# The low parts of w_out and of the experts' weights, from GpSimd to VectorE

## The chip, the cores and the metric

The kernel runs on one core of a Trainium2 chip. The metric is device time in microseconds (us) of one execution. Names used below: PE is TensorE (matmuls), DVE is VectorE, ACT is ScalarE, POOL is GpSimd, SP is SyncE, which here issues the DMAs from HBM. GpSimd issues the indirect DMAs (gathers and stores by token number) itself.

## What is computed

Three layers in a row, in float32: a gated linear attention, a mixture of experts with a capacity of 384 tokens per expert, and a dense feed-forward layer.

```python
# attention, per batch and head (4 x 8 x 768 x 48)
state = f[:, :, t, :, None] * state + k_t (outer) v_t;  y[:, :, t] = q_t @ state
# experts: N=3072 tokens, D=384, E=8, F=1024; tokens are taken in order of logit, 384 each
for e in range(E):
    h = np.maximum(x[mask] @ w1[e], 0.0)
    out[mask] = h @ w2[e]
# dense layer, d_ff=2048
h = x @ w_in
g = h * np.clip(h + 3.0, 0.0, 6.0) / 6.0
return g @ w_out
```

w_in and w_out arrive as float64; the other tensors as float32.

## The kernel before

**Precision.** Each float32 matrix of the feed-forward part is kept as two: a rounded "high part" (float32r, made by a copy on ACT) and a "low part", the difference between the value and its high part. A product is three matmuls: high x high, low x high, high x low (`run_passes`, L672 to L675; `wih`/`wil`, `woh`/`wol{g}`, `w1h`/`w1l`, `w2h`/`w2l`, `xh`/`xl`, `hh`/`hl`). `split_raw` (L668) makes both parts: L669 the copy on ACT, L670 the subtraction on the engine that it is given.

**Stages.** First attention with the routing's first steps (to about 213 us), in which w_in is also prepared; then eight expert stages, one per expert, in which the 384 tokens of an expert go through w1, w2, w_in and w_out (`Experts.ffn_`: l1, l2, l3, l4). An expert stage is a generator of some 144 ticks; a tick is one `run_passes`, three matmuls of 128x128 by 384 columns. After every tick the main loop (L978 to L989) lets other generators go one step, so their instructions land in the engines' queues between the expert's own. Queues run in program order; there is no planner, the order is that of the ticks.

**What runs beside the first expert.** `w0` is `load_weights(0)`, the rest of expert 0's weights: one step on every even tick. `out_parts` is `prep_out`, a `narrowed` generator over 16 pieces of w_out (128x384): one step on every odd tick. A piece's steps: `L872` `absolute` of the next piece on ACT, `L882`, `L884`, `L886`, `L889` on DVE (float64 words to float32), `split_raw` with its low part on GpSimd, and `fetch(i+2)`, a load on SP into the buffer `pw` (two buffers, so it waits until the low part of piece i has read its buffer). Eight steps of `out_parts` are taken ahead of the stage (`GAP`). `ap` is the routing of the next experts: DVE operations and small PE matmuls in turn (`q_ge`, `q_ok`, `q_qc`, L450 to L660).

**What runs beside every expert but the last.** `load_weights(n+1)`, from tick 42 or as soon as the expert's number is known, one step every 4 to 6 ticks (`wp`): 14 pieces (six of w1, 128x512; eight of w2, 128x384), each `split_raw` with the low part on GpSimd and `fetch(i+WLAG)` into `wst` (three buffers, WLAG=3). Expert 0's first four low parts are on DVE (`W0_DVE`). What steps are left at the end of a stage are run then. `gather(n+1)` issues three indirect loads on GpSimd; `make_x` transposes the tokens; l4's end issues three indirect stores on GpSimd.

**The expert's own vector work.** In l1 `L771` (ACT, `hh`) and `L772` (DVE, `hl`, two ticks later); in l3 `L805` (ACT), `L806` (DVE, `ga`), `L808` (ACT, `hh`), `L809` (DVE, `hl`), one block of four operations per six ticks; between l2 and l3 `L790` (ACT, `xh`) and `L791` (DVE, `xl`).

Of the kernel before, what the change touches and what calls it, by code (L numbers as in the profile page):

```python
# [10 lines left out]
F32=mybir.dt.float32; F32R=mybir.dt.float32r; BF=mybir.dt.bfloat16; I32=mybir.dt.int32; U32=mybir.dt.uint32  # L11
# [654 lines left out]
DM=384; F1=1024; F2=2048  # L666

def split_raw(nc, raw, hi, lo, eng_lo):  # L668
    nc.scalar.copy(hi, raw)  # L669
    eng_lo.tensor_tensor(out=lo, in0=raw, in1=hi.bitcast(F32), op=OP.subtract)  # L670
# [6 lines left out]
W0_DVE=(0,1,2,3); WLAG=3  # L677

class Experts:
# [15 lines left out]
    def load_weights(s,k):  # L695
        nc=s.tc.nc
        e=nc.sync.value_load(s.rt.eid[k][0:1,0:1],min_val=0,max_val=7)
        w1h=s.ew.tile([128,3,F1],F32R,name="w1h"); w1l=s.ew.tile([128,3,F1],F32R,name="w1l")
        w2h=s.ew2.tile([128,8,DM],F32R,name="w2h"); w2l=s.ew2.tile([128,8,DM],F32R,name="w2l")
        s.W[k]=((w1h,w1l),(w2h,w2l))  # L700
        jobs=[]
        for hf in range(2):
            for d in range(3):
                c=slice(hf*512,(hf+1)*512)
                jobs.append((s.w1[bass.ds(e,1),d*128:(d+1)*128,c].rearrange("a p f -> p (a f)"),w1h[:,d,c],w1l[:,d,c],512))
        for g in range(8):
            jobs.append((s.w2[bass.ds(e,1),g*128:(g+1)*128,:].rearrange("a p m -> p (a m)"),w2h[:,g],w2l[:,g],DM))
        got=[]; big=[]
        def fetch(i):
            src,_,_,n=jobs[i]  # L710
            if k>0 or i in (9,10): t=s.act.tile([128,512],F32,name="wst",bufs=WLAG)
            elif i<6:
                if i%2==0: big.append(s.act.tile([128,3,DM],F32,name=["xh","xl","xh"][i//2]).rearrange("p a b -> p (a b)"))
                t=big[i//2][:,(i%2)*512:(i%2)*512+512]
            else: t=big[1 if i<9 else 2][:,(i-6)%3*DM if i<9 else (i-11)*DM:][:,:DM]
            nc.sync.dma_start(t[:,:n],src)
            got.append(t[:,:n])
        for i in range(WLAG if k else 6): fetch(i)
        yield
        for i,(_,hi,lo,n) in enumerate(jobs):  # L720
            yield
            split_raw(nc,got[i],hi,lo,nc.vector if k==0 and (i in W0_DVE) else nc.gpsimd)
            for j in ([i+WLAG] if k else {3:(6,7,8,9,10),5:(11,12,13)}.get(i,())):
                if j<len(jobs): fetch(j)
    def gather(s,k):
        nc=s.tc.nc; ids=s.rt.ids[k]
        xg=s.act.tile([128,3,DM],F32,name="xg",bufs=1)
        for h in range(3):
            nc.gpsimd.indirect_dma_start(out=xg[:,h],out_offset=None,in_=s.x,in_offset=bass.IndirectOffsetOnAxis(ap=ids[:,h:h+1],axis=0))
        s.xg=xg  # L730
# [115 lines left out]
def gla_moe_ffn(tc,q,k,v,f_logit,moe_w_gate,moe_w1,moe_w2,moe2_w_in,moe2_w_out,out):  # L846
    nc=tc.nc
    with ExitStack() as ctx:
# [9 lines left out]
        def narrowed(pool,jobs,W,work,places):  # L858

            words=jobs[0].dtype!=F32  # L860
            got={}; mag={}
            def fetch(i):
                if i>=len(jobs): return
                n=jobs[i].shape[-1]
                w=pool.tile([128,W,2],U32,name="pw",bufs=2)
                if not words: w=w.rearrange("p c t -> p (c t)")[:,:n].bitcast(F32)
                nc.sync.dma_start(w.rearrange("p c t -> p (c t)") if words else w,jobs[i].bitcast(U32) if words else jobs[i])
                got[i]=w
            def absolute(i):
                if not words or i>=len(jobs): return  # L870
                mag[i]=work(i)
                nc.scalar.activation(mag[i],got[i][:,:,1].bitcast(F32),AF.Abs)  # L872
            fetch(0); fetch(1)
            yield
            absolute(0)
            for i in range(len(jobs)):
                yield
                r=got[i]
                if words:
                    V=nc.vector  # L880
                    lw,hw=got[i][:,:,0],got[i][:,:,1]; m=mag[i]; t=m.bitcast(U32)
                    V.tensor_scalar(m,m,2.0**-15,None,op0=OP.max)  # L882
                    yield
                    V.tensor_scalar(t,t,3,0x3ffffff8,op0=OP.logical_shift_left,op1=OP.bitwise_and)  # L884
                    yield
                    V.scalar_tensor_tensor(t,hw,0xC0000000,t,op0=OP.bitwise_and,op1=OP.bitwise_or)  # L886
                    yield
                    absolute(i+1)
                    V.scalar_tensor_tensor(lw,lw,29,t,op0=OP.logical_shift_right,op1=OP.bitwise_or)  # L889
                    r=lw.bitcast(F32)  # L890
                hi,lo=places(i)
                split_raw(nc,r,hi,lo,nc.gpsimd)
                fetch(i+2)
        def prep_in(pool):
            cc=lambda i: slice(i%4*512,i%4*512+512)
            return narrowed(pool,[moe2_w_in[i//4*128:i//4*128+128,cc(i)] for i in range(12)],512,
                            lambda i: pool.tile([128,512],F32,name="pm",bufs=2),
                            lambda i: (wih[:,i//4,cc(i)],wil[:,i//4,cc(i)]))
# [44 lines left out]
        def pools(c):  # L943
            act=c.enter_context(tc.tile_pool(name="act",bufs=2))
            pf=c.enter_context(tc.tile_pool(name="pf",bufs=4,space=PS))
            pa=c.enter_context(tc.tile_pool(name="pa",bufs=1,space=PS))
            rt.ps=c.enter_context(tc.tile_pool(name="pr",bufs=1,space=PS))
            return Experts(tc,rt,moe_w1,moe_w2,x_dram,out,ident,(wih,wil),(woh,wol),(ew,ew2,act,pf,pa))
        with ExitStack() as c:
            ex=pools(c)  # L950
            po=c.enter_context(tc.tile_pool(name="po",bufs=1))
            out_parts=prep_out(po)
            next(out_parts); w0=None
            rt.bank=None
            for i,_ in enumerate(p0):
                if got: break
                if known and w0 is None: w0=ex.load_weights(0); next(w0)
                ex.warm(WP[min(i,len(WP)-1)])
                for _ in range(GAP.get(i,0)): next(out_parts)
            ex.gather(0)  # L960
            for _ in range(3): next(w0)
            for _ in range(GAP['ids']): next(out_parts)
            for _ in range(4): next(w0)
            ex.warm(WARM2)
            ex.make_x0(WARM3)
            for _ in range(W0N): next(w0)
            def all_phases():
                for _ in p0: yield
                for n in range(1,E):
                    for w in rt.phase(n):  # L970
                        for _ in range(w): yield
            ap=all_phases()
            def spread(g):
                for w in g:
                    for _ in range(w): yield
            for n in range(E):
                wgen=xgen=None; gat=n+1>=E; gi=None; last=n+1>=E
                for i,_ in enumerate(ex.ffn(n)):  # L978
                    if n==0:
                        if i%2==0: next(w0,None)  # L980
                        else: next(out_parts,None)
                    if not (PAUSE if n else PAUSE0)[0]<=i<(PAUSE if n else PAUSE0)[1] and (n or i>=P1): next(ap,None)
                    if last: continue
                    if wgen is None and len(known)>n+1 and i>=W_SLOT: wgen=ex.load_weights(n+1); wi=i; wp=max(WPMIN,min(WPMAX,(138-i)//15))
                    if not gat and len(got)>n+1 and i>=30:
                        ex.gather(n+1); gat=True; gi=i
                    if xgen is None and gat and i>=min(max(gi+X_LAG,X_SLOT),122): xgen=spread(ex.make_x(n+1))
                    if xgen is not None: next(xgen,None)
                    if wgen is not None and (i-wi)%wp==0: next(wgen,None)  # L989
                if not last:  # L990
                    while len(got)<=n+1: next(ap)
                    if not gat: ex.gather(n+1)
                    if wgen is None: wgen=ex.load_weights(n+1)
                    for _ in wgen: pass
                    if xgen is None: xgen=spread(ex.make_x(n+1))
                    for _ in xgen: pass
# [39 lines left out]
```

## Time and profile before

| | |
|---|---|
| median of 3 runs | 896.9 us (895.48 to 900.68) |
| the profiled execution | 900.39 us, its span 898.7 us |
| mean granted TensorE clock in it | 0.968 |
| PE busy | 837.9 us, 93% |
| DVE busy | 534.9 us, 60% |
| ACT busy | 371.1 us, 41% |
| POOL busy | 307.8 us, 34% |

Busy times are unions of an engine's instructions in the profiled execution. In the rows further down a timeline row is: start and duration in us, engine, line of the kernel, operation, output<-input, shape, count; in brackets how long the engine stood idle before it and what it waited for. In a table by stretches each engine has its busy us and, in brackets, its instructions; then the granted PE clock (1.00 is full), the DMA engines' busy share and GB/s. A table of waits has the waiting engine and instruction, what released it, total us, number of waits and the longest.

### The profile page before, as it was taken

To read this page: it belongs to the slowest core of one execution; us is meant where nothing else is said; L and a number is where in the kernel's file an instruction comes from. 1 tells how busy PE (TensorE), PEld (TensorE's weight loads), DVE (VectorE), ACT (ScalarE), POOL (GpSimd) and SP (SyncE) were. 2 spreads that over 40 slices of the span, in tenths; PEclk is the share of its full clock that TensorE was granted. 3 is DMA by queue.
4 is the path that set the end of the run, shared out by engine and by line. 5 is a ranking of instruction groups with operands and counts; after the bars stand their busy time and mean duration, and the time that the engine had idled before them with its cause. 6 is when DMAs were issued, how large, how long until landed. Compare 5 with 4: busy or idle time off the path is not lost.

```text
span 898.7 us, 16095 instructions
## 1 busy us (share of the span) xinstructions
PE 837.9 (93%) x6086; PEld 788.9 (88%) x6086; DVE 534.9 (60%) x1369; ACT 371.1 (41%) x741; POOL 307.8 (34%) x378
## 2 busy tenths in 40 slices
PE   7998889896987699999999999999999999999995
PEld 5887778786877699989999999999999999999995
DVE  7989799567768844674574565555674422431331
ACT  4655556424234441542354144316423541642331
POOL 7677566316213540432133133313330440331001
PEclk9999899977999899999999999999999999999998
DMA  8775686026123411120221112201220220110000
GB/s 257 189 167 125 172 237 144 29 78 187 53 71 101 119 62 37 63 71 27 74 62 33 63 62 63 71 27 58 61 77 12 75 91 18 60 47 27 1 1 31
DMA packets 77158, 71.91 MB, mean 80 GB/s; under 512 B 29200, under 2 KB 65040, under 8 KB 77072
## 3 DMA queue, kind: packets, MB, share of 16 engines
q1 hardware_dynamic: 74000, 61.37, 24.0%
q0 software_dynamic: 3072, 9.44, 3.3%
q8 instruction: 49, 0.80, 0.4%
q14 instruction: 37, 0.30, 0.1%
HBM read 61.35 MB, written 9.44 MB: 79 GB/s over the span
## 4 chain that ended last, share of the span: by engine, by line
PE 57%; issue 14%; DVE 7%; ACT 2%; POOL 2%; DMA 2%; SPq 0%; POOLq 0%; ACTq 0%; DVEq 0%
PE pF L673 9%; PE acc L673 9%; PE pF L675 8%; PE pF L674 8%; PE acc L675 8%; PE acc L674 8%; POOL wol L670 1%; DVE ga L806 1%; PE pM L195 1%; PE pA L135 1%; DMA pw<-in_moe_w_out_dram 1%; PE pY L169 1%; PE pY L163 1%; PE acc L383 1%; POOL out_dram L838 1%
## 5 line engine op out<-in xcount | busy, mean ns | idle before, releaser
L806 DVE SCALAR_TENSOR_TENSOR ga<-ga,pF 128x384 f32<-128x384 f32 x128 | 70.7, 552 | 109.5 <-ACT ga L805 109.3
L673 PE MATMUL pF<-xh,wih 128*128 128x384 f32 x384 | 133.3, 347 | 1.9 <-ACT xh L790 1.9
L673 PE MATMUL acc<-woh,hh 128*128 128x384 f32 x384 | 134.2, 349 | 0.0
L675 PE MATMUL pF<-xl,wih 128*128 128x384 f32 x384 | 131.3, 342 | 0.0
L674 PE MATMUL pF<-xh,wil 128*128 128x384 f32 x384 | 130.9, 341 | 0.0
L674 PE MATMUL acc<-woh,hl 128*128 128x384 f32 x384 | 130.0, 339 | 0.9 <-DVE hl L809 0.9
L675 PE MATMUL acc<-wol,hh 128*128 128x384 f32 x384 | 130.0, 338 | 0.0
L670 POOL TENSOR_TENSOR w1l<-wst,w1h 128x512 fp32r<-128x512 f32 x42 | 55.6, 1323 | 173.9 <-ACT w1h L669 173.9
L805 ACT ACTIVATE ga<-pF,three 128x384 f32<-128x384 f32 x128 | 74.1, 579 | 99.2 <-PE pF L675 99.1
L809 DVE TENSOR_TENSOR hl<-ga,hh 128x384 fp32r<-128x384 f32 x128 | 72.8, 569 | 60.2 <-ACT hh L808 59.9
L808 ACT CAST hh<-ga 128x384 fp32r<-128x384 f32 x128 | 65.7, 513 | 104.0 <-DVE ga L806 104.0
L670 POOL TENSOR_TENSOR w2l<-wst,w2h 128x384 fp32r<-128x384 f32 x58 | 59.9, 1035 | 111.5 <-ACT w2h L669 111.5
L771 ACT ACTIVATE hh<-pF 128x384 fp32r<-128x384 f32 x64 | 31.4, 492 | 123.1 <-PE pF L675 111.9
L772 DVE SCALAR_TENSOR_TENSOR hl<-pF,hh 128x384 fp32r<-128x384 f32 x64 | 35.5, 555 | 75.1 <-ACT hh L771 74.8
L673 PEld LDWEIGHTS pF<-xh,wih 128*128 128x128 f32 x384 | 73.0, 190 | 2.3 <-ACT xh L790 2.2
L674 PEld LDWEIGHTS acc<-woh,hl 128*128 128x128 f32 x384 | 72.7, 189 | 1.3 <-DVE hl L809 1.3
L675 PEld LDWEIGHTS pF<-xl,wih 128*128 128x128 f32 x384 | 73.3, 191 | 0.4 <-DVE xl L791 0.3
L674 PEld LDWEIGHTS pF<-xh,wil 128*128 128x128 f32 x384 | 73.2, 191 | 0.0
L673 PEld LDWEIGHTS acc<-woh,hh 128*128 128x128 f32 x384 | 72.7, 189 | 0.1
L675 PEld LDWEIGHTS acc<-wol,hh 128*128 128x128 f32 x384 | 72.6, 189 | 0.0
L673 PE MATMUL pF<-xh,w1h 128*128 128x384 f32 x192 | 67.8, 353 | 0.6 <-ACT xh L741 0.6
L675 PE MATMUL acc<-hl,w2h 128*128 128x384 f32 x192 | 64.5, 336 | 3.0 <-DVE hl L772 3.0
(286 smaller groups left out, 1766.8 us busy)
## 6 DMA issues: line engine op xcount, KB each, us to landing
wst<-in_moe_w_dram SPq DMA_DIRECT2D x58, 192.0 KB, 2.4
wst<-in_moe_w_dram SPq DMA_DIRECT2D x42, 256.0 KB, 2.7
pw<-in_moe_w_in_dram SPq DMA_DIRECT2D x12, 512.0 KB, 4.0
pw<-in_moe_w_out_dram SPq DMA_DIRECT2D x16, 384.0 KB, 3.1
v<-in_v_dram SPq DMA_DIRECT2D x24, 192.0 KB, 5.2
x_dram<-y SPq DMA_DIRECT2D x24, 192.0 KB, 3.6
fr<-in_f_logit_dram SPq DMA_DIRECT2D x7, 576.0 KB, 5.4
kr<-in_k_dram SPq DMA_DIRECT2D x7, 576.0 KB, 5.6
```

The source lines that it names most:

```text
L135: nc.tensor.matmul(pA[j][s][:,p],KH[u][r,p,c*C:(c+1)*C],QT[u][r,p,c*C:(c+1)*C],start=True,stop=True)
L163: for r in rows: nc.tensor.matmul(PY[j][p//2][r,p],St[j%2][r,p],QT[u][r,p,cc],start=p==0 or last and p==2,stop=False)
L670: eng_lo.tensor_tensor(out=lo, in0=raw, in1=hi.bitcast(F32), op=OP.subtract)
L673: nc.tensor.matmul(out, ahi, bhi, start=start, stop=False)
L674: nc.tensor.matmul(out, alo, bhi, start=False, stop=False)
L675: nc.tensor.matmul(out, ahi, blo, start=False, stop=stop)
L771: nc.scalar.activation(hh,p,AF.Relu)
L772: s.defer(2,lambda: nc.vector.scalar_tensor_tensor(hl,p,0.0,hh.bitcast(F32),op0=OP.max,op1=OP.subtract))
L805: nc.scalar.activation(a,p,AF.Relu,bias=s.three[:,0:1])
L806: late(f,1,lambda: nc.vector.scalar_tensor_tensor(g,a,6.0,p,op0=OP.min,op1=OP.mult))
L808: late(f,1,lambda: nc.scalar.copy(gh,g))
L809: late(f,3,lambda: nc.vector.tensor_tensor(out=gl,in0=g,in1=gh.bitcast(F32),op=OP.subtract))
```

## The change

Low parts go from GpSimd to DVE, one step behind the copy on ACT that makes the high part:

- in `load_weights`, a step makes piece i's high part (ACT) and piece i-1's low part (DVE), and then issues the load that waits for that low part; one more step at the end makes the last low part. Expert 0's first six pieces stay as they were (four on DVE, two on GpSimd).
- in `narrowed`, the 16 pieces of w_out (`W==DM`) take one step more each: copy, `yield`, low part on DVE and load. The 12 pieces of w_in, during attention, keep GpSimd.
- in the main loop `out_parts` goes one step on every odd tick and on every sixteenth (0, 16, ...).

```diff
@@ load_weights
+        def low(i):
+            _,hi,lo,n=jobs[i]
+            nc.vector.tensor_tensor(out=lo,in0=got[i],in1=hi.bitcast(F32),op=OP.subtract)
+            for j in ([i+WLAG] if k else ()):
+                if j<len(jobs): fetch(j)
         for i,(_,hi,lo,n) in enumerate(jobs):
             yield
-            split_raw(nc,got[i],hi,lo,nc.vector if k==0 and (i in W0_DVE) else nc.gpsimd)
-            for j in ([i+WLAG] if k else {3:(6,7,8,9,10),5:(11,12,13)}.get(i,())):
-                if j<len(jobs): fetch(j)
+            if k==0 and i<6:
+                split_raw(nc,got[i],hi,lo,nc.vector if i in W0_DVE else nc.gpsimd)
+                for j in {3:(6,7,8,9,10),5:(11,12,13)}.get(i,()): fetch(j)
+            else:
+                nc.scalar.copy(hi,got[i])
+                if i>(0 if k else 6): low(i-1)
+        yield
+        low(len(jobs)-1)
@@ narrowed
-                split_raw(nc,r,hi,lo,nc.gpsimd)
-                fetch(i+2)
+                if W!=DM:
+                    split_raw(nc,r,hi,lo,nc.gpsimd)
+                    fetch(i+2)
+                else:
+                    nc.scalar.copy(hi,r)
+                    yield
+                    nc.vector.tensor_tensor(out=lo,in0=r,in1=hi.bitcast(F32),op=OP.subtract)
+                    fetch(i+2)
@@ gla_moe_ffn
                         if i%2==0: next(w0,None)
-                        else: next(out_parts,None)
+                        if i%2 or i%16==0: next(out_parts,None)
```

## Rows read from the trace of the kernel before

**Rows 1.** Busy times by stretch: first expert in four, then the second.

```profile
213.65:235.00 21.35, 16.50 (x77) 15.18 (x77) 20.56 (x51) 7.25 (x16) 10.73 (x10) 0.84 0.26 81
235.00:282.20 47.20, 41.36 (x235) 37.51 (x236) 31.19 (x89) 18.68 (x40) 8.62 (x9) 0.96 0.22 67
282.20:313.40 31.20, 20.31 (x114) 18.72 (x112) 28.64 (x72) 12.92 (x27) 17.07 (x14) 0.87 0.45 133
313.40:329.17 15.77, 15.77 (x86) 14.53 (x86) 7.37 (x20) 8.30 (x20) 8.59 (x10) 0.83 0.17 51
329.17:412.08 82.91, 81.51 (x497) 77.81 (x497) 48.83 (x141) 31.07 (x63) 23.83 (x26) 1.00 0.17 53
```

**Rows 2.** PE's waits in the first expert's stage, 213.65 to 329.17.

```profile
PE pR L462 <- DVE q_ge L450: 8.4, 4, 5.4
...
PE acc L675 <- DVE hl L772: 3.0, 1, 3.0
...
PE pR L630 <- DVE q_qj L627: 0.3, 1, 0.3
```

**Rows 3.** PE's waits from 329.17 to 880.

```profile
PE pR L462 <- DVE q_ge L450: 1.4, 1, 1.4
...
PE pR L452 <- DVE q_qc L464: 0.7, 1, 0.7
```

**Rows 4.** Timelines of GpSimd and DVE in A.

```profile
214.09 1.97 POOL L670 TENSOR_TENSOR w2l<-xl,w2h 128x384 fp32r<-128x384 f32 x2 [1.26 <-ACT w2h L669]
...
214.11 1.02 DVE L574 TENSOR_TENSOR q_oh<-r_e,q_ec 128x16 bf16<-128x16 f32 x1
...
217.21 0.18 DVE L579 TENSOR_TENSOR q_nw<-q_nw,q_ec 128x24 f32<-128x24 f32 x1
...
232.18 1.06 DVE L884 TENSOR_SCALAR wol<-wol 128x384 uint32<-128x384 uint32 x1
```

**Rows 5.** Timelines of DVE, GpSimd and PE in C.

```profile
283.10 0.35 DVE L882 TENSOR_SCALAR wol<-wol 128x384 f32<-128x384 f32 x1
...
285.10 1.27 DVE L605 SCALAR_TENSOR_TENSOR q_sl<-q_inc,pR,q_mem 128x24 int32<-128x24 f32 x1
...
303.67 4.21 DVE L882 TENSOR_SCALAR wol<-wol 128x384 f32<-128x384 f32 x1
...
303.20 1.32 POOL L670 TENSOR_TENSOR w1l<-wst,w1h 128x512 fp32r<-128x512 f32 x1
...
306.66 0.99 POOL L670 TENSOR_TENSOR w2l<-wst,w2h 128x384 fp32r<-128x384 f32 x1
...
311.59 0.23 PE L462 MATMUL pR<-q_oh,q_ge 128*128 128x32 bf16 x2 [5.42 <-DVE q_ge L450]
```

**Rows 6.** ACT's longest wait in the first expert's stage.

```profile
ACT wol L872 <- DMA pw<-in_moe_w_out_dram: 26.5, 10, 4.1
```

**Rows 7.** Timelines of GpSimd, ACT and PE in B.

```profile
236.15 1.03 POOL L670 TENSOR_TENSOR wol<-pw,woh 128x384 fp32r<-128x384 f32 x1 [3.14 <-ACT woh L669]
...
257.03 1.15 POOL L670 TENSOR_TENSOR wol<-pw,woh 128x384 fp32r<-128x384 f32 x1 [4.10 <-ACT woh L669]
...
240.45 0.55 ACT L872 ACTIVATE wol<-pw 128x384 f32<-128x384 f32 x1 [3.99 <-DMA pw<-in_moe_w_out_dram]
...
252.26 0.44 PE L673 MATMUL pF<-xh,wih 128*128 128x384 f32 x1 [1.90 <-ACT xh L790]
```

**Rows 8.** Timeline of DVE: its subtractions of 384 and of 512 columns.

```profile
364.37 0.56 DVE L809 TENSOR_TENSOR hl<-ga,hh 128x384 fp32r<-128x384 f32 x1 [0.58 <-ACT hh L808]
364.85 0.55 DVE L806 SCALAR_TENSOR_TENSOR ga<-ga,pF 128x384 f32<-128x384 f32 x1
...
208.93 1.41 DVE L670 TENSOR_TENSOR w1l<-xl,w1h 128x512 fp32r<-128x512 f32 x2
```

**Rows 9.** Timeline of DVE in the second expert's stage.

```profile
387.72 1.36 DVE L809 TENSOR_TENSOR hl<-ga,hh 128x384 fp32r<-128x384 f32 x1
```

**Rows 10.** Timeline of DVE ahead of the first expert.

```profile
199.22 0.81 DVE L559 SCALAR_TENSOR_TENSOR q_base<-q_mx,q_st,q_b 128x1 f32<-128x1 f32 x1
```

## The prediction

> **What bounds the kernel now.** The page's busy shares come first (the table above): PE is busy 93% of the span, DVE 60%, GpSimd (POOL) 34%. Work moved from GpSimd to DVE can only pay where PE is not full, so the next view is the one by stage [rows 1]. In the second expert's stage PE is full (81.51 of 82.91 us). The first expert's, 213.65 to 329.17, takes 115.5 us, 32.6 us more. I cut it into A (213.65 to 235), B (to 282.2), C (to 313.4) and D (to 329.17). DVE fills A (20.56 of 21.35 us) and C (28.64 of 31.2), has 16 us free in B, and half of D. The table of PE's waits in that stage [rows 2] says who is late: ten rows, 21.9 us in all, of which 18.7 end with DVE (8.4 on `q_ge`, 3.0 on `hl`, seven rows down to 0.3), 2.5 with ACT, 0.7 with a DMA. For the rest of the kernel the same table has three rows, 3.0 us [rows 3].
>
> Why is DVE late? Two things stand in the timelines. In A [rows 4] a comparison of 128x16 takes 1.02 us, a subtraction's neighbour of 128x24 only 0.18. The slow one lies beside a GpSimd low part (two in 1.97 us from 214.09) and ends with it. Ten such stand in A, from 214.11 to 232.18; against the same lines elsewhere they cost 7.6 us. In C there are six [rows 5], from `L605` (1.27 us) to `L882`, which takes 0.35 us at 283.10 and 4.21 us at 303.67, while GpSimd runs four low parts in a row from 303.20 to 307.65. All six cost 7.9 us. PE then waits 5.42 us, and its granted clock is 0.87 in C and 0.83 in D, for a part of the time the lower of its two levels (1.2 instead of 2.4 GHz) [rows 1].
>
> The second thing is a loop in B. ACT's queue stops at `L872` for the next piece of w_out: 26.5 us in ten waits in this stage [rows 6]. That load starts only when GpSimd has read the buffer: its low part ends at 237.18, `L872` starts at 240.45, 3.27 us later [rows 7]. Five low parts from 236.15 to 257.03 are 5.22 us apart; 1.03 of it is the low part, and the remaining 0.92 `L872` and the copy. The program wants one each 8 ticks of the expert's loop; the second expert runs its 144 ticks in 82.91 us, 0.576 each, so 8 take 4.6 us. The loop is slower than PE, and ACT holds everything behind it (`hh`, `xh`, `ga`): PE's 1.90 us wait for `xh` before 252.26 is of this kind.
>
> **The change, part by part.** GpSimd loses low parts of 1.03 us (384 columns) and 1.32 us (512), which nobody waits for except through these two effects. DVE gains for each 128x384 0.48 us (it takes 0.56, but the next instruction starts 0.48 later), for each 128x512 0.70 us (two in 1.41) [rows 8]. The first stage gets 15 of w_out (7.2 us), 8 of expert 0 (3.8) and 14 of expert 1 (6x0.70+8x0.48=8.0): 19 us, against 15.7 us of stretching that goes (7.6+7.9, and 0.2 in B). DVE's total hardly moves. What counts is where it falls.
>
> A: out 7.6; in 8 of expert 0 (3.8), two of w_out (1.0), two more preparation steps from the doubled call at ticks 0 and 16 (0.9, of 0.35 to 0.55 each). I give the stage's end the net, -1.9. Ends: 0 (the lows queue ahead of `hl` and `q_ge`, for which PE waits) and -3.5 (the 3.0 us wait goes, and some of the slow clock, 0.84 in A).
>
> B: the loop becomes 0.92 (`L872`, copy) + 0.55 (low part, if DVE gets to it in time) + 3.27 (load) = 4.7 us. The program now gives a job 5 steps at 9 per 16 ticks, 8.9 ticks, 5.1 us at 0.576. So ACT's waits should nearly vanish. PE has 41.36 us of work in these 47.2, and the slow clock (0.96) is worth 1.9 of it: at best -7.7. DVE's work rises from 31.2 to 36.8 (8 lows 3.8, four more steps 1.8); were its idle 16 us all to stay, B would be 52.8, +5.6. I take -4, a B of 43.2 us with DVE 85% full, since the rows in which DVE idles there follow ACT's waits for the load.
>
> C: out 7.9, in four lows of w_out (1.9), two steps (0.9), seven of expert 1 (4.7): -0.4. Ends -4 (the single stall ahead of the 5.42 us wait weighs more than spread lows) and +2 (the chain through `q_ge` meets several lows). D: 7 us of lows and late steps on DVE's 7.37, in 15.77 us, hidden behind PE's matmuls, whose l4 inputs are made four blocks ahead; if that cover is gone, +2. Its clock was lost in C's long stall; all of it would be 2.7 us (0.17 of 15.77), I take -1.
>
> Experts 2 to 7: 8 us of lows per stage on a DVE that is busy 48.83 of 82.91 us, each queued one step (4 to 6 ticks) behind its copy, so it seldom waits; behind it stand `ga`, `hl` and the routing. The stretched rows are there too: `hl` 1.36 us at 387.72 [rows 9], and behind it PE's longest wait of these stages, 1.4 [rows 3]. Of the 3.0 us I take half: -1.5 (ends -3 and +1.5). An expert's load is issued one step later, since SP waits for DVE's low part: two steps, at least 8 ticks or 4.6 us, are left for 256 KB where w_out's 384 KB take 3.27, so nothing; one that misses holds ACT's queue for about 1 us. The step more at the end of expert 1's weights falls behind the first stage's last tick; those columns are used some 40 ticks later: nothing.
>
> Ahead of the stage: `L559`, on the path to the first token list, takes 0.81 us beside a low part [rows 10], where a 128x24 operation takes 0.18 [rows 4]: -0.6. The third w_out load is issued some 8 us later, behind DVE's low part and so beside the first gather; at worst it takes half of its 3.27 us from it, +1.5. Together 0. GpSimd's later gathers and stores lose the low parts queued ahead of them; PE's one wait on a gather in the first stage is 0.7 us: nothing.
>
> Sum: -1.9-4-0.4-1-1.5+0 = -8.8 us. Against the profiled execution, 900.39 us (span 898.7), that is 891.6; that execution lies 3.5 us above the median of 896.9, and from the median the sum gives 888.1. I say **889.5**, near the mean of the four executions (898.4) less the sum.
>
> On the lock itself: the Trainium skill, "SBUF — State Buffer", section "Who interferes with whom", says that DVE and GpSimd hold a shared port pair for one whole instruction while the other blocks. Read so, `L882` would have lost at most the rest of one low part, about 1.3 us, and C 5.4 us in all instead of 7.9, so that C would end 2.5 us worse than my term, an estimate inside its ends. The row shows four low parts long, and I keep the row.
>
> **Rivals.** *DVE is the new bound (slower).* Place: B. If the 16 us that DVE idles there are latency (`ga` to `hh` to `hl` pass through ACT) and not the loop, the added 5.6 us lie end to end with the rest. It decides from the point where DVE's idle time in B stays above 10.4 us (47.2-36.8). At the full 16: B +5.6, A -1.9, C +1, D +2, rest 0, so +6.7: about 905. For it: DVE already ends most of PE's waits, and 19 us are more than 15.7. Against it: ACT's 26.5 us of waits for the load. On its side, in a sentence apart: the Trainium skill, "Perfetto Trace Analysis", section "Optimizing Scalar/DVE Operations", advises taking work off a saturated DVE, to GpSimd too, though it doubts the gain because the two share a port; this change goes the other way.
>
> *Even trade (no change).* A and C give their 2.3 us, B's shorter loop is eaten by DVE's queue, the clock stays: -2 to -4, 893 to 897.
>
> *More than forecast.* The stalls were also what dropped the clock, and B runs at PE's pace: -3.5-7.7-4-2.7-3 = -20.9, some 878.
>
> **How the numbers follow.** Forecast case (882 to 892) 0.46, more 0.12, even trade 0.25, slower 0.17. A measurement of this kernel tells about 0.5% (4.5 us) from no change: faster than 892.4 0.58, between 0.25, above 901.4 0.17. The ends of all terms add to about -21 and +13; the range, 877 to 903, takes in the best case and leaves out part of the slower one.
>
> **What would show it.** Right: no DVE row on 128x24 or less above 0.3 us after 214; `L882` at 0.35 us everywhere; ACT's waits for the w_out load far below 26.5 us; PE's waits in the first stage down from 21.9 to about 13; that stage near 108 us, DVE some 3 us busier in it. Wrong: DVE over 90% busy through B and PE waiting longer for `q_ge` and `hl` there, or ACT's waits for the load unchanged because DVE reaches the low part late.

## The result and the profile after

| | before | after |
|---|---|---|
| median | 896.52 us (895.48 to 900.68) | 887.62 us (887.29 to 888.67) |
| ratio after/before | | 0.9899, interval 0.9868 to 0.9929 |
| the profiled execution, its span | 900.39, 898.7 us | 887.29, 885.6 us |

The changed kernel is 1.0% faster, 8.9 us by the medians; the sum in the prediction was 8.8. The terms of that sum are another matter, and most of what follows is about them.

The first part of the profile's page of the kernel after has each engine's busy time, share of the span and instructions. GpSimd falls from 307.8 to 169.5 us, DVE rises from 534.9 to 566.4, PE is busy 94%:

```profile
PE 831.6 (94%) x6086; PEld 783.5 (88%) x6086; DVE 566.4 (64%) x1491; ACT 372.4 (42%) x741; POOL 169.5 (19%) x256
```

The table by stretches of the kernel after, columns as in [rows 1]: the first expert's stage cut at its matmul passes 23, 88 and 122 (A to D), then the second expert's.

```profile
210.02:228.71 18.69, 16.54 (x78) 15.28 (x79) 17.89 (x62) 7.08 (x16) 0.00 (x0) 0.80 0.18 55
228.71:274.41 45.70, 40.56 (x227) 37.01 (x228) 32.33 (x92) 18.26 (x37) 0.00 (x0) 0.93 0.21 64
274.41:302.61 28.20, 20.25 (x122) 18.63 (x122) 25.26 (x80) 13.27 (x27) 2.96 (x4) 0.95 0.49 148
302.61:319.11 16.50, 15.30 (x86) 14.06 (x86) 13.63 (x35) 9.53 (x22) 1.33 (x3) 0.88 0.24 71
319.11:400.46 81.35, 81.35 (x497) 77.75 (x497) 51.28 (x156) 31.26 (x63) 6.39 (x10) 1.00 0.18 54
```

To compare equal work, the kernel before is cut at the same passes here (the cuts of [rows 1] lie within 1.3 us of these):

```profile
213.65:235.27 21.62, 16.71 (x78) 15.31 (x79) 20.72 (x51) 7.43 (x17) 10.73 (x10) 0.84 0.25 80
235.27:280.98 45.71, 39.92 (x227) 36.16 (x228) 30.46 (x87) 17.50 (x38) 8.62 (x8) 0.96 0.23 70
280.98:313.39 32.41, 21.52 (x121) 19.93 (x121) 29.20 (x74) 13.92 (x29) 17.08 (x14) 0.87 0.43 128
313.39:329.17 15.78, 15.78 (x86) 14.54 (x86) 7.38 (x20) 8.31 (x20) 8.59 (x10) 0.83 0.17 51
```

All lengths in the table below are differences of such starts, read from PE's timeline of each profiled execution; "2 to 7" runs from the start of the second stage to the start of the eighth.

| kernel | A | B | C | D | stage | 2 to 7 |
|---|---|---|---|---|---|---|
| before | 21.6 | 45.7 | 32.4 | 15.8 | 115.5 | 483.0 |
| after | 18.7 | 45.7 | 28.2 | 16.5 | 109.1 | 480.0 |

Three stretches fall: A by 2.9, C by 4.2, the later stages by 3.1. B, from which the prediction took the largest term, doesn't move at all (at a granted clock of 0.93 instead of 0.96), and D is 0.7 longer. That makes 9.5 us. DVE's busy time falls by 2.8 us in A and by 3.9 in C, nearly as much as these stretches themselves. The two spans differ by 13.1. Of the rest, 4.3 us lie in the attention part, whose instructions the change doesn't touch (its last `L200` copy starts at 188.73 before and at 184.40 after), and 0.7 us go the other way between that copy and the stage's start. The median difference of 8.9 fits 9.5 less 0.7.

PE's waits in the kernel after, first in the first expert's stage (210.02 to 319.11, three of nine rows, 16.9 us in all; ten rows and 21.9 us before, of which [rows 2] has three), then in all later ones, where one row of 0.3 us is left of three with 3.0 [rows 3]:

```profile
PE pR L462 <- DVE q_ge L450: 6.9, 5, 1.9
PE pR L452 <- DVE q_qc L464: 2.7, 3, 1.2
PE pF L760 <- DMA xg<-x_dram,q_ids: 1.8, 2, 1.2
...
PE pR L452 <- DVE q_qc L464: 0.3, 1, 0.3
```

In the kernel after, lines from `L735` on have numbers higher by 10: its `L892` is `L882` of before, `L882` is `L872`, `L899` is `L889`; `L906` and `L908` are the copy and the low part of w_out, `L731` and `L722` those of the experts.

The stretched DVE rows of A and C are gone. The timeline of DVE after has the same instructions as [rows 4], [rows 5] and [rows 10]: the comparison of 128x16 in 0.17 instead of 1.02 us, `L605` in 0.24 instead of 1.27, the clamp of w_out (`L892`) in 0.35 instead of 4.21, `L559` in 0.22 instead of 0.81. In PE's timeline the wait of 5.42 us for `q_ge` in C is gone; the longest two for it there are now 1.49 and 1.29.

```profile
194.15 0.22 DVE L559 SCALAR_TENSOR_TENSOR q_base<-q_mx,q_st,q_b 128x1 f32<-128x1 f32 x1
...
211.88 0.17 DVE L574 TENSOR_TENSOR q_oh<-r_e,q_ec 128x16 bf16<-128x16 f32 x1
...
277.54 0.24 DVE L605 SCALAR_TENSOR_TENSOR q_sl<-q_inc,pR,q_mem 128x24 int32<-128x24 f32 x1
...
300.00 0.35 DVE L892 TENSOR_SCALAR wol<-wol 128x384 f32<-128x384 f32 x1
...
300.14 0.24 PE L462 MATMUL pR<-q_oh,q_ge 128*128 128x32 bf16 x2 [1.29 <-DVE q_ge L450]
...
302.54 0.23 PE L462 MATMUL pR<-q_oh,q_ge 128*128 128x32 bf16 x2 [1.49 <-DVE q_ge L450]
```

In B nothing got quicker. The table of ACT's waits in the first stage after has 20.8 us at the load of w_out, where [rows 6] has 26.5. ACT's timeline after has three starts of `L882` (the wait for the next load of w_out), DVE's has the low parts of the same pieces:

```profile
ACT wol L882 <- DMA pw<-in_moe_w_out_dram: 20.8, 10, 5.1
...
229.63 0.56 ACT L882 ACTIVATE wol<-pw 128x384 f32<-128x384 f32 x1 [3.29 <-DMA pw<-in_moe_w_out_dram]
...
236.73 0.55 ACT L882 ACTIVATE wol<-pw 128x384 f32<-128x384 f32 x1 [5.08 <-DMA pw<-in_moe_w_out_dram]
...
241.39 0.55 ACT L882 ACTIVATE wol<-pw 128x384 f32<-128x384 f32 x1 [3.29 <-DMA pw<-in_moe_w_out_dram]
...
231.51 0.55 DVE L908 TENSOR_TENSOR wol<-pw,woh 128x384 fp32r<-128x384 f32 x1
...
237.75 0.56 DVE L908 TENSOR_TENSOR wol<-pw,woh 128x384 fp32r<-128x384 f32 x1 [2.25 <-ACT woh L906]
...
242.78 0.56 DVE L782 SCALAR_TENSOR_TENSOR hl<-pF,hh 128x384 fp32r<-128x384 f32 x1 [1.99 <-ACT hh L781]
243.25 0.55 DVE L908 TENSOR_TENSOR wol<-pw,woh 128x384 fp32r<-128x384 f32 x1
```

The low parts start 6.24 and 5.50 us apart here, and seven of them from 231.51 to 268.18 are 6.1 us apart; GpSimd's eight in B, from 236.15 to 276.77, were 5.8 apart. The prediction's loop was 4.7. Two things were missing in it: the low part at 243.25 stands in DVE's queue behind `hl` (242.78), which waits for ACT, and the load after the low part at 231.51 (done at 232.06) is there for ACT only at 236.73, 4.67 us later instead of 3.27. The distance of 6.1 us does not say by itself that the loop sets B's pace: B's 65 ticks take 0.70 us each, so the 8.9 ticks per piece of the new program are 6.2 us, and the 8 ticks of the kernel before are 5.6. The pieces keep step with the ticks in both.

### The profile page after: what moved, and what is told of

Same layout as the page of the kernel before. It is cut to its first block, busy times and chain, and to the rows that moved or that the text cites. A ratio compares the mean times of both kernels' runs of the same rounds, so it can differ in the third digit from the quotient of the medians.

```text
span 885.6 us, 15975 instructions
## 1 busy us (share of the span) xinstructions
PE 831.6 (94%) x6086; PEld 783.5 (88%) x6086; DVE 566.4 (64%) x1491; ACT 372.4 (42%) x741; POOL 169.5 (19%) x256
## 4 chain that ended last, share of the span: by engine, by line
PE 59%; issue 10%; DVE 9%; DMA 3%; ACT 3%; POOL 1%; SPq 0%; POOLq 0%; ACTq 0%; DVEq 0%
PE acc L673 9%; PE pF L673 9%; PE acc L675 9%; PE acc L674 9%; PE pF L675 9%; PE pF L674 9%; DMA pw<-in_moe_w_out_dram 2%; DVE ga L816 1%; PE pM L195 1%; DVE hl L819 1%; PE pA L135 1%; ACT ga L815 1%; PE pY L169 1%; PE pY L163 1%; POOL out_dram L848 1%
## 5 line engine op out<-in xcount | busy, mean ns | idle before, releaser
L848 POOL DMA_INDIRECT out_dram<-ga,q_ids x24 | 23.7, 989 | 430.5 <-ACT ga L846 427.4
L673 PE MATMUL acc<-hh,w2h 128*128 128x384 f32 x192 | 65.9, 343 | 0.6 <-ACT hh L781 0.6
L674 PE MATMUL pF<-xh,w1l 128*128 128x384 f32 x192 | 65.4, 341 | 0.0
```

The costliest lines, as they stand in the source:

```text
L673: nc.tensor.matmul(out, ahi, bhi, start=start, stop=False)
L674: nc.tensor.matmul(out, alo, bhi, start=False, stop=False)
L848: st=nc.gpsimd.indirect_dma_start(out=s.out,out_offset=bass.IndirectOffsetOnAxis(ap=ids[:,t:t+1],axis=0),in_=o,in_offset=None)
```

## The experiments

The theory at the outset: GpSimd's reads of SBUF hold DVE, so it pays to take its low parts away, and w_out's low parts pay most, through the loop in B. The rivals: the gain is that of the experts' low parts alone; or what counts is who computes the low part in time, and not who reads beside DVE. Each ratio is against the kernel before on the same chip (897.2 us for the first four, 896.7 for the next four, 897.5 for the last three). The kernel after has its own such ratio, 0.9899, and is best compared with them by it.

**One: the low parts of w_out alone.** The experts' low parts go back to GpSimd.

```diff
 in load_weights, against after
-                nc.scalar.copy(hi,got[i])
-                if i>(0 if k else 6): low(i-1)
+            split_raw(nc,got[i],hi,lo,nc.vector if k==0 and (i in W0_DVE) else nc.gpsimd)
```

> Only w_out's low parts go to DVE; the experts' stay on GpSimd as in the kernel before. Theory (a stretched DVE row beside a GpSimd low part is what the change removes): the stretched rows beside the experts' low parts come back, 7 of 10 at the start of the first stage, most of those before the long stall, and PE's waits of 3.0 us in the later stages; 887.6 +2 +3 +2.7, so 893 to 896. Rival (what counts is w_out's loop through ACT and its steadier steps, not the stretching): the whole gain is here already, 887 to 889.

Measured: 899.95 us, ratio 1.0028 (1.0004 to 1.0051). Both theories missed: this half of the change gives nothing and costs a little. By the table of stretches of this kernel, D (its last quarter) has DVE at 12.37 us and takes 18.03, where before it took 15.78. Part of that is PE's granted clock, 0.76 instead of 0.83, which this one execution doesn't separate from DVE's part:

```profile
310.46:328.49 18.03, 16.89 (x86) 15.48 (x86) 12.37 (x28) 9.55 (x22) 8.08 (x9) 0.76 0.15 45
```

**Two: the experts' low parts alone.** w_out stays on GpSimd, at odd ticks.

```diff
 in narrowed and in the main loop, against after
-                    nc.scalar.copy(hi,r)
-                    yield
-                    nc.vector.tensor_tensor(out=lo,in0=r,in1=hi.bitcast(F32),op=OP.subtract)
+                split_raw(nc,r,hi,lo,nc.gpsimd)
...
-                        if i%2 or i%16==0: next(out_parts,None)
+                        else: next(out_parts,None)
```

> Only the experts' low parts go to DVE; w_out keeps GpSimd and its odd ticks. Theory: the stretching beside the experts' low parts is gone, what remains stands beside single w_out low parts (1.03 us each, every 5 us): 889 to 891, with PE's waits after the first stage near 0.3 us. Rival (w_out's steps are what counts): 894 to 897, the first stage as long as before (115 us).

Measured: 887.48 us, ratio 0.987 (0.9834 to 0.9907). That is the whole gain, and somewhat better than expected. PE's waits behind the first stage are down to the same single row as in the kernel after:

```profile
PE pR L452 <- DVE q_qc L464: 0.3, 1, 0.3
```

**Three: GpSimd's reads put back, with nothing using their result.** Beside each copy of an expert's high part, GpSimd subtracts that part from itself into the place of the low part, and DVE then writes the true one.

```diff
 in load_weights, against after
                 nc.scalar.copy(hi,got[i])
+                h=hi.bitcast(F32)
+                nc.gpsimd.tensor_tensor(out=lo,in0=h,in1=h,op=OP.subtract)
```

> The changed kernel, and beside each expert piece's copy GpSimd subtracts the high part from itself into the low part's place, before DVE writes the real one there: GpSimd reads SBUF again as long and as often as it did before, while DVE keeps all the low parts and nothing else waits for GpSimd. Theory (GpSimd's reading holds DVE up): the stretched rows are back on a DVE that has more to do than before, 896 to 900, and some 4 to 7 us in the first stage and 3 in the later ones. Rival (it was the place of the work in the queues, not the sharing): 887.6 to 889.

Measured: 905.32 us, ratio 1.0079 (1.0047 to 1.0112), 17.7 us above the kernel after (some 16 by the ratios), and above the kernel before too. The direction is the theory's; the size is larger than the 8.4 to 12.4 us that were expected. The timelines of GpSimd and DVE in this kernel show why: `L733` is the added subtraction, and a DVE low part (`L910`) that starts beside it takes 1.40 instead of 0.55 us.

```profile
291.16 1.16 POOL L733 TENSOR_TENSOR w1l<-w1h 128x512 fp32r<-128x512 f32 x1 [4.76 <-ACT w1h L731]
...
291.33 1.40 DVE L910 TENSOR_TENSOR wol<-pw,woh 128x384 fp32r<-128x384 f32 x1
```

In this stage DVE is busy 100.0 us instead of 89.1, with the same operations, and the stage is 10.9 us longer; stages 2 to 7 are 5.6 longer. A small part of it is another thing: DVE's own low part now waits for GpSimd's, 1.2 us in this stage. The added instruction also writes SBUF, so this run doesn't tell GpSimd's reads from its writes.

**Four and five: ACT no longer stands at the load.** In a piece's steps of w_out, `absolute(i+1)`, which waits for the next load, is moved behind this piece's copy: in the kernel before behind the low part and the load too, in the kernel after right behind the copy.

```diff
-                    absolute(i+1)
+                    if W!=DM: absolute(i+1)
... four, against before
                 split_raw(nc,r,hi,lo,nc.gpsimd)
                 fetch(i+2)
+                if W==DM: absolute(i+1)
... five, against after
                     nc.scalar.copy(hi,r)
+                    absolute(i+1)
                     yield
```

> The kernel before, with one instruction moved: of w_out's steps ACT's absolute value of the next piece stands behind the copy of this piece, not ahead of it, so that a low part and the next load no longer wait for the load in between. Theory of the loop (ACT's 26.5 us of waits for w_out's load set the middle part of the first stage): ACT's waits fall under 8 us and that part gets 4 us shorter, 892 to 893. Rival (that part is set by the routing's round trips between PE and DVE's queue; ACT's waits are slack): only PE's 1.9 us wait for xh goes, 894.5 to 896.5.

Measured: 895.6 us, ratio 0.9967 (0.9946 to 0.9988). ACT's wait for the load falls in this stage from 26.5 us [rows 6] to 0.7, and B from 45.7 to 41.4 us, as the theory has it. But ACT now waits 32.7 us for DVE's part of the piece (10.4 before), and the table of PE's waits of this stage keeps three long ones on DVE, which in PE's timeline lie in A (`hl`, at 225.04) and in C (`q_ok` at 288.23, the longest `q_ge` at 308.16):

```profile
PE pR L462 <- DVE q_ge L450: 8.5, 4, 5.1
PE pR L624 <- DVE q_ok L618: 5.5, 1, 5.5
PE acc L675 <- DVE hl L772: 4.1, 1, 4.1
...
ACT woh L669 <- DVE pw L889: 32.7, 12, 7.8
...
ACT wol L872 <- DMA pw<-in_moe_w_out_dram: 0.7, 2, 0.4
```

So the loop was real in the kernel before: 4.3 us in B and in the stage, 3.0 us (1.1 to 4.8) of the whole by the ratio, 1.6 by the medians. PE's idle time in B falls from 5.8 to 2.3 us at the same granted clock (0.96). The time alone settles nothing: the median lies in the rival's range, while the 3.0 us of the ratio would lie between the two ranges.

> The changed kernel, with ACT's absolute value of w_out's next piece behind the copy of this piece instead of ahead of it. Theory (in the changed kernel the loop is still there, because DVE comes late to the copy and to the low part, so the middle part of the first stage kept its 45.7 us): ACT's waits for w_out's load fall from 20.8 to under 8 us and the middle part is 4 us shorter, as it was in the kernel before (45.7 to 41.4 us in its profile): 883 to 885 us. Rival (with all low parts on DVE its queue sets that part): 886.5 to 888.5.

Measured: 889.88 us, ratio 0.9925 (0.99 to 0.995); the kernel after has 0.9899, and both expectations were lower. Here the same move gives nothing. ACT's wait for the load is gone from its list but for 0.5 us, and its wait at DVE's step before the copy, 12.8 us in the kernel after, has grown by more:

```profile
ACT woh L906 <- DVE pw L899: 35.7, 15, 6.8
...
ACT wol L882 <- DMA pw<-in_moe_w_out_dram: 0.5, 1, 0.5
```

PE's idle time in B stays (5.1 us after, 5.4 here), so the load is no longer what PE waits for there. DVE is late there for both: within B ACT waits 18.6 us at DVE's step, where it waited 10.3 in number four, and all 5.3 us of PE's waits in B end with DVE's routing (`q_qc`, `q_ge`, `q_fj`).

**Six: the third load of w_out out of the first gather's way.**

```diff
 in narrowed, against after
+                    if W==DM and i==1: fetch(2)
...
-                    fetch(i+2)
+                    if i: fetch(i+2)
```

> The changed kernel, but the third load of w_out, which the change put beside the first gather (2.75 us after the token list, where it stood 5 us ahead of it), is issued at the first tick of the first expert. Theory (the load takes DMA time from the gather): the stage starts 8.5 us after the token list instead of 10.6, 885.5 to 886.5. Rival (the gather's own landing varies by as much; kernels with the early load started 8.5, 10.2 and 10.6 us after the list): 887 to 888, start still about 10 us after it.

Measured: 888.22 us, ratio 0.9905 (0.9872 to 0.9937): no change. From the first token list to the stage's start it takes 9.60 us here and 10.56 in the kernel after, and over the profiled executions of all kernels from 8.5 to 11.6. The load may be a part of that: the five kernels in which it is issued 2.4 to 2.8 us after the list (after, one, three, five, nine) take 10.6 to 11.6, the other eight 8.5 to 10.6, a difference of 1.3 us between the means of single executions. The median of this kernel is too uncertain to show it.

**Seven: two and four together**, the experts' low parts on DVE, w_out on GpSimd with `absolute` last (the two edits as above).

> Only the experts' low parts on DVE (887.5 us), and w_out's copy ahead of the absolute value of the next piece; w_out's low parts stay on GpSimd. Theory of the loop: the middle part falls from 44.1 to about 41 us, 883.5 to 885. Rival (a gain in the middle part is given back in the next, where DVE is full): 886.5 to 888.

Measured: 886.09 us, ratio 0.9879 (0.9832 to 0.9927). The lowest median of kernels that compute everything, but it can't be told from the kernel after or from number two. What B gains (43.1 us against 44.1 in number two) C gives back (30.4 against 29.0). The time lies between the two expectations.

**Eight, ten and eleven: the experts' part taken to pieces.** Against the kernel before, only expert 1's low parts (eight), only those of experts 2 to 7 (ten), only expert 0's last eight (eleven) go to DVE.

```diff
 in load_weights, against before; k>=2 and k==0 in the other two
+        if k==1:
...
+        else:
             for i,(_,hi,lo,n) in enumerate(jobs):
                 yield
                 split_raw(nc,got[i],hi,lo,nc.vector if k==0 and (i in W0_DVE) else nc.gpsimd)
```

> The kernel before, with only expert 1's 14 low parts on DVE, the ones that are made during the first stage. Theory (three low parts that piled up on GpSimd behind the gathers held one DVE instruction for 4.2 us just ahead of PE's longest wait): the third part of the first stage is 3 to 4 us shorter, 892.5 to 894.5. Rival (the sum of what DVE loses and gets there, -7.9+7.5 us, counts): no change, 896 to 898.

Measured: 893.73 us, ratio 0.9975 (0.9948 to 1.0001), in the theory's range, though the interval just touches no change. This run doesn't part theory from rival: the rival's 7.5 us include 2.8 for low parts and steps of w_out, which this kernel leaves as they were, and without them the sum gives -3.2 us too. C takes 29.3 instead of 32.4 us, DVE's busy time in it falls by as much (29.20 to 25.87), and the clamp that took 4.21 us ([rows 5], here `L899`) takes 0.82 beside what is left of GpSimd's work there:

```profile
298.61 0.82 DVE L899 TENSOR_SCALAR wol<-wol 128x384 f32<-128x384 f32 x1
```

> The kernel before, with the low parts of the weights of experts 2 to 7 alone moved to VectorE; w_out and experts 0 and 1 keep GpSimd, so the first expert's stage is as before. Theory: the later stages give what their profile showed in the whole change, PE's waits there falling from 3.0 to 0.3 us; against 896.7 that is 893 to 894.5. Rival: that gain came with the first stage's (routing that is ahead when the stage begins), so that here it stays at PE's waits of 3.0 us and 896 to 897.5.

Measured: 895.08 us, ratio 0.9972 (0.9949 to 0.9995), which is 2.4 us below its 897.5; the theory had 2.2 to 3.7 below its 896.7, the rival nothing. The trace puts it where the theory does. Stages 2 to 7 take 480.0 us as in the kernel after, the first stage 115.3 as before, and of PE's waits behind it the one row of 0.3 us is left.

> The kernel before, with the eight late low parts of expert 0's weights alone moved to VectorE, one step behind their copies; all other low parts stay on GpSimd. Theory: the first 23 passes of the first expert's stage fall by 2 to 3 us, as in the whole change, and the rest of the stage keeps it: 893.5 to 895 us. Rival: the next stretch, which waits for VectorE whatever comes before it, takes it back: 896 to 897.5.

Measured: 894.03 us, ratio 0.9953 (0.9933 to 0.9973), the theory's range. A takes 19.0 us instead of 21.6 and the rest of the stage keeps it. The three ratios multiply to 0.9900: the kernel after has 0.9899, and number two, which is all three at once, lies within its interval of it. Each ratio is uncertain by 0.002 to 0.003, so the better evidence is in the traces: A -2.7 (eleven), C -3.1 (eight) and stages 2 to 7 -3.1 (ten) are what number two has together, -2.7, -3.4 and -3.1. The gain is the sum of three separate places.

**Nine: less work on DVE in B.** Two of DVE's four steps for a piece of w_out are left out of the kernel after.

```diff
-                    V.tensor_scalar(m,m,2.0**-15,None,op0=OP.max)
+                    if W!=DM: V.tensor_scalar(m,m,2.0**-15,None,op0=OP.max)
...
-                    V.tensor_scalar(t,t,3,0x3ffffff8,op0=OP.logical_shift_left,op1=OP.bitwise_and)
+                    if W!=DM: V.tensor_scalar(t,t,3,0x3ffffff8,op0=OP.logical_shift_left,op1=OP.bitwise_and)
```

> The kernel after, in which VectorE leaves out two of the four operations of each w_out piece (the clamp L892, 0.35 us, and the shift L894, 0.35 to 0.55 us), so that w_out is not converted as the reference needs it; the steps stay where they are. That takes about 0.7 us of VectorE for each of 15 pieces, some 10 us, out of the first expert's stage, half of it out of the middle stretch (passes 23 to 88). Theory: VectorE's queue sets the pace of that stretch and of the next in the changed kernel, so that w_out's low parts put on it cost what they saved; then the middle stretch falls from 45.7 to 42.5 to 44 us, and the time to 881 to 885 us. Rival: the stretch is set by the distance in ticks between the routing's matmuls and VectorE's answers, whatever VectorE's load; then the time stays at 886.5 to 888.5.

Measured: 886.28 us, ratio 0.9856 (0.9815 to 0.9898). The time lies between the two expectations, and its interval overlaps that of the kernel after, so it settles nothing. Nor does the trace, for B. B takes 44.0 us (45.7), A 17.6 (18.7), C 27.2 (28.2), and PE's waits for `q_ge` fall from 6.9 to 5.3 us. B in this kernel's table of stretches:

```profile
234.59:278.63 44.04, 38.09 (x227) 34.77 (x228) 28.33 (x78) 17.57 (x36) 0.00 (x0) 1.00 0.22 71
```

DVE is 7.8 us less busy in this stage (81.3 against 89.1), and the stage is 3.8 us shorter. But in B PE's granted clock was 1.00 instead of 0.93: PE's busy time there is 2.5 us less (38.09 against 40.56), which is more than B's 1.7, and PE's idle time even rose from 5.1 to 6.0. So B's gain is the clock's as far as this trace goes. A is another matter: DVE idles only 0.8 us there in both kernels, and its busy time and the stretch both fall by 1.1 us. In C PE is as busy as it was (20.27 against 20.25) and idles 1.1 us less. That the rest of B is distance (matmul, DVE, matmul) is argued, not shown. (This profiled execution's span is 888.9 us, since its attention part took 6 us more than that of the kernel after.)

The stretches of all these kernels, read as in the first table:

| kernel | A | B | C | D | stage | 2 to 7 |
|---|---|---|---|---|---|---|
| one: w_out alone | 22.0 | 45.1 | 31.2 | 18.0 | 116.4 | 483.1 |
| two: experts alone | 19.0 | 44.1 | 29.0 | 15.6 | 107.7 | 479.9 |
| three: GpSimd reads | 23.8 | 44.3 | 33.0 | 18.8 | 120.0 | 485.6 |
| four: before, copy first | 21.8 | 41.4 | 33.3 | 14.7 | 111.2 | 483.1 |
| five: after, copy first | 19.1 | 44.5 | 28.7 | 16.9 | 109.2 | 479.9 |
| six: third load later | 18.7 | 45.5 | 28.1 | 16.5 | 108.7 | 479.9 |
| seven: two and four | 18.9 | 43.1 | 30.4 | 15.8 | 108.2 | 479.9 |
| eight: expert 1 | 21.7 | 43.9 | 29.3 | 15.3 | 110.2 | 483.1 |
| nine: two steps less | 17.6 | 44.0 | 27.2 | 16.5 | 105.3 | 480.0 |
| ten: experts 2 to 7 | 21.7 | 45.6 | 32.5 | 15.6 | 115.3 | 480.0 |
| eleven: expert 0 | 19.0 | 44.3 | 32.4 | 15.9 | 111.6 | 483.1 |

B also moves by up to 1.8 us in kernels that change none of its instructions (eight and eleven), so a difference of that size in B carries little alone. A and C follow DVE's work: in these thirteen profiled executions DVE's idle time is 0.8 to 1.6 us in A and 2.8 to 4.7 in C, while A goes from 17.6 to 23.8 us and C from 27.2 to 33.3.

## Why the prediction was right, and where it was not

The time, 887.6 us, lies near the forecast of 889.5, and the reason given first, stretched DVE rows beside GpSimd's reads, is the one that the runs bear out: number two, three and the three parts show it from both sides. But of the terms only A's and the one ahead of the stage came near; B's was 4 us too good, those of C, D and the later stages were together 3.7 us too bad (-2.9 forecast, -4.2+0.7-3.1 = -6.6 measured). That the total came out, 8.8 forecast and 8.9 measured, is luck: these two cancel.

- **A**, -1.9 (ends 0 and -3.5), measured -2.9. The mechanism and the bounds held: DVE is full in A, so A falls with its busy time, by 2.8 us (20.72 to 17.89). The net of what DVE loses and gains was the right measure and 0.9 us too small; one of its terms, two more preparation steps, was one. Number eleven gives -2.7 by expert 0's low parts alone.
- **B**, -4, measured 0.0. This is the step that failed. The prediction read ACT's 26.5 us at the load as time on the path, and made it vanish with a loop of 4.7 us. The pieces came 6.1 us apart, with the low part late in DVE's queue in places, and ACT's waits for the load in this stage only fell to 20.8 us. The prediction had named as a sign of being wrong that they stay because DVE is late; most of them did. Number four shows that the loop was worth 4.3 us in B of the kernel before. Number five shows that after the change it is worth little: with the wait for the load gone PE idles in B as before. What PE waits for there is DVE's routing: 4.5 of its 5.1 us of waits in B end with `q_ge` (1.8), `q_qc` (1.6) and `q_fj` (1.1); before, 1.9 of 5.7 ended with ACT's `xh`. Why DVE's answers come later than in number four isn't shown. A second slip stands in the same step: at the prediction's own 8.9 ticks a piece B's 65 ticks hold 7.3 pieces, not 8 and four more steps. Seven low parts and three steps fewer fell in it, DVE's work rose by 1.9 us and not 5.6, and the pieces left over went into C and D.
- **C**, -0.4 (ends -4 and +2), measured -4.2, just outside. The measure held here too: DVE's busy time in C fell by 3.9 us (29.20 to 25.26). The sum was mis-sized. The 7.9 us of stretching went; in came four low parts of w_out and six, not seven, of expert 1, and three preparation steps fewer instead of two more, since w_out's pieces come later now. The favourable end of the prediction had another reason, that the single stall of 3.9 us weighs more because it lies right ahead of PE's longest wait. The -4.2 don't need it, and no run shows it apart from the sum: in number eight C falls by 3.1 us and DVE's busy time by 3.3.
- **D**, -1, measured +0.7. PE's clock is 0.88 instead of 0.83, so a part of the expected gain is there, but the stretch now has waits of its own (PE is busy 15.30 of 16.50 us, where it was full). DVE has 13.63 us there instead of 7.38: the case "if that cover is gone" in the prediction. The waits come with w_out's low parts: PE idles 1.1 to 2.3 us in D in the six profiled kernels that make them on DVE, and not at all in the other seven. C and D belong together, since six preparation steps moved into D: -1.4 forecast, -3.5 measured.
- **Stages 2 to 7**, -1.5 (ends -3 and +1.5), measured -3.1. PE's waits there [rows 3] fell from 3.0 to 0.3 us, not by half.
- **Ahead of the stage**, 0. `L559` gave its 0.59 us as worked out. The load beside the gather can't be seen in the time (number six); its profiles leave room for about 1 us. The 4.3 us of the attention part are not the change's.

w_out's low parts bring nothing on DVE: number one (0.3% slower) and the equal times of number two and of the kernel after show it. The reason is in part argued: DVE loses the stretching by them and gets their 0.48 us each in the stage where its queue is longest. D's waits are the part that the traces show.

Of the rivals, *DVE is the new bound* was priced at the point where DVE's idle time in B stays above 10.4 us. It did stay above (13.4 us: 45.70 less 32.33), and B still got no longer, since DVE's work there rose by 1.9 us, not 5.6. Half of that rival is true: most of PE's waits in B end with DVE. The *even trade* is what B and w_out's part did; *more than forecast* had the C of -4 and the later stages of -3 right and B wrong.

On the lock the row was right to be kept. The Trainium skill, "SBUF — State Buffer", section "Who interferes with whom", has an engine hold the shared ports for a whole instruction. Read as one instruction at most, `L882` would have lost about 1.3 us, an estimate from a low part's length. It lost 3.9 beside four low parts, and takes 0.35 us with none beside it. That section also says that a GpSimd instruction that reads SBUF contends with a DVE instruction of two SBUF inputs; number three agrees (0.55 to 1.40 us), though it can't tell reads from writes.

The Trainium skill's "Perfetto Trace Analysis", section "Optimizing Scalar/DVE Operations", considers moving work off a busy DVE, to GpSimd among others, and doubts it because of the ports. DVE is busy 90 to 96% in A and C here, and the doubt is what the measurement bears out: taking work from GpSimd onto it gained 1.3% in number two, putting GpSimd's work back beside it cost 1.8% by the ratios in number three.

What stays open: why B takes 45.7 us and not PE's 40.6, since DVE's queue and the distance between matmul and answer are both left as reasons once the load is gone (number five), and the profiled execution of number nine, meant to part them, had B at another clock; and whether the 0.2% between the kernel after and number seven is real.

## What to carry to other kernels

Work on GpSimd that reads SBUF is priced by what it does to DVE, not by its own duration: look in DVE's timeline for the same small line at 0.17 and at 1 us. In a stretch that DVE nearly fills (here A and C) the net of its busy time is the price, so count which instructions will really fall into that stretch: a changed step pattern moves them across its ends. A wait of another engine (here 26.5 us on ACT) is a gain only if what it hands on is late for something, so follow it to the next queue before it enters a sum. Before a shorter stretch is put down to an edit, compare the granted clock in it (here 1.00 and 0.93). When a change has two halves, price and run each alone: one half here gave everything.

## What the runs showed that was not expected

A DVE instruction can lose the time of several GpSimd instructions in a row: 4.21 us beside four for one that takes 0.35 alone. In the kernel before, operations on 128x1 or 8x8 elements take 0.8 to 1.0 us (`L643`, `L644`, `L651` in A) and 0.15 to 0.16 in the kernel after. The trace of before had this already; that it goes when GpSimd's low parts go is what the runs add.

The attention part, in which PE, ACT, DVE and GpSimd have the same instructions in the same order in all thirteen kernels, ends between 184.4 and 190.4 us in their profiled executions, so 6 us of a span say nothing about a change made behind it. These ends go with PE's granted clock: up to there it was at its lower level for 0 us in the kernel after, 10.2 in the kernel before and 13.7 in number nine, and all of this lies in the first 100 us, whose mean granted clock is 1.00, 0.95 and 0.93. In the rows of the granted clock, in 40 slices of 22 us (kernel after, then number nine), this is slice 5 from the left; slices 9 and 10, which differ too, begin at 177 us and lie for the most part behind the attention.

```profile
PEclk9999999978999899999999999999999999999998
...
PEclk9999899985999899999999999999999999999998
```
